# A recurrent mixer with an MLP on one core: v streamed twice in the diagonal products, new planner numbers, q and k loaded earlier

## The chip, the core and the metric

The kernel runs on one core of a Trainium2 chip. The metric is the time on the device of one execution, in microseconds (us). The engines of the core are TensorE (PE in the profile, its weight loads PEld), VectorE (DVE), ScalarE (ACT), GpSimd (POOL) and SyncE (SP), which issues nearly all DMAs here.

## What is computed

An mLSTM layer (4 batches, 8 heads, 768 steps, head width 40) is followed by a mixer over the sequence and an MLP of width 320 to 1280 to 320, all in float32.

```python
for t in range(S):
    m_new = np.maximum(f_gate[:, :, t] + m, i_gate[:, :, t])
    f_stab = np.exp(f_gate[:, :, t] + m - m_new)
    i_stab = np.exp(i_gate[:, :, t] - m_new)
    C = f_stab[..., None] * C + i_stab[..., None] * np.einsum('bhd,bhe->bhde', vt, kt)
    n = f_stab * n + i_stab * kt
    h_tilde = np.einsum('bhde,bhe->bhd', C, qt)
    denom = np.maximum(np.abs(np.einsum('bhd,bhd->bh', n, qt)[:, :, None]), 1.0)
    y[:, :, t] = o * h_tilde / denom          # o = sigmoid(o_gate)
u = x + (x.T @ U @ V).T                       # x: y with the heads side by side
out = u + np.maximum(u @ w_ch1, 0.0) @ w_ch2
```

## The kernel before, in words

The recurrence is computed in chunks of 128 steps. A sequence is cut into two halves of 384 steps (`hf`), a half into three chunks, and the heads into groups of 3, 3 and 2. `gates()` runs the scalar recurrence of all 32 rows once per half: a scan for m (`gate_max`, L415), the exponentials (`gate_exp`, `gate_input_exp` on ACT), two more scans (`gate_w` L445, `gate_g` L453), and small products on PE that turn the results (`gate_turn`, L466) and spread the totals (`totals`).

`attention(b, base)` does, for each head of a half:
- `scores`: k times q for three chunks, for two heads at once in the two halves of PE's rows, six matmuls with 40 rows and 128 columns each (in the trace `ps<-qk`, and each float32 matmul is two MATMUL records);
- `decay` (`ps<-fhl,idsel`) or `load_decay` (`fd<-fsd`, a DMA): a row of forget factors on all partitions;
- `decay_scan` (L779, DVE), which makes the 128x128 decay triangles, and `weigh` (L783, DVE), scores times decay into `wt`;
- `pv`: the diagonal products, three matmuls `ps<-tk,wt` with the weights `wt` (128 by 128) and v with a column of ones as the moving operand, 41 columns.

For each head group `kv` (`ps<-v,tk`) makes the state of each chunk, `kv_mask` (L699) and `state` (L713) carry it on, `inter` (`ps<-C,q`) adds what comes from earlier chunks, and `norm`, `out_norm` and `gate` write x. `rows` and `cols` apply U and V, and `mlp(b, hf)` runs ten row blocks of `up` (`ps<-ut,w1h` and `w1l`, 384 columns), `relu_high` (ACT L947), `relu_low` (DVE L949) and `down` (`ps<-w2h,h` and `w2l`, 320 columns). The MLP operands are split in a high and a low part; the weights are unpacked from float64 words by DVE (`weight_shift` L531, `weight_sign` L533, `weight_tail` L535).

The order on every engine is made by a planner (`Plan`) while the kernel is built. Each piece of work is an `op` with a priority, an engine, a cost and its dependencies; `ORDER` adds to the priority by kind, `ORDER0` adds more for batch 0 (`p.batch == 0`). Of what can start first on an engine, the piece with the lowest priority number is taken. SP issues the DMAs in this order, and a DMA whose buffer is still held blocks those behind it. `dma(nbytes)` gives the planned time of a transfer. Where the plan finds PE idle, or finds that PE would stream fewer than `TICK_COLUMNS` columns in a slice `TICK` of its time, `keep_busy` puts in fillers: matmuls of a tile of zeros, 256 columns of bf16 (`ps<-zeros`), that nobody reads. `load` tells the planner which share of a piece's time counts as streaming. The fillers are in the program as fixed instructions: if PE gets there late, they run all the same. Every matmul goes through the helper `mm`, so in the trace they all stand under L296.

```python
while FORCE:
    n = int(start // TICK)
    left = (n + 1) * TICK - start
    gain = 2.4 / (2 if start < COLD else 1)
    lack = TICK_COLUMNS - busy[n] - load * gain * min(cost, left)
    if lack <= gain * max(0.0, left - cost) or left < FILL_NS or not filler(start):
        break
```

Of the kernel before, what the change touches and what calls it, by code (L numbers as in the profile page):

```python
# [20 lines left out]
P = 128  # L21
# [3 lines left out]
DV = D + 1  # L25
# [19 lines left out]
BF_FROM = 64  # L45
LAG = 2
CV0, CV1, CV2 = 53.6, 80.0, 95.3
TICK, TICK_COLUMNS, FILL_NS, FILL_COLUMNS = 5120.0 / 3, 2000.0, 107.0, 256.0
RP, MP = 75.4, 175.5
GP = 21.3  # L50
ALT_PRI = 94.9
FILL_SLACK, FORCE, FILL_TO = 0.8, True, 4096.0

ORDER = {
    "gate": 20.0, "gate_w": 10.0, "part2": -70.0, "out_norm": -30.0, "part1": -10.0, "gate_turn": 10.0, "part3":
    -30.0, "rest1": 2.0, "w_low": 30.0, "vi": -10.0, "state": -4.0, "qk_low": -10.0, "load_tk": -20.0, "w13_low":
    -30.0,
}
ORDER0 = {
    "rows": 25.0, "inter": 3.0, "x_low": -10.0, "weigh": 10.0,  # L60
}
BEGIN, COLD = 600.0, 7000.0
DELTA = {"pe": 0}

WIDE_DMA = 630.0
PLAIN = 222.0


SLOTS = {
# [203 lines left out]
def mlstm_mixer_kernel(  # L273
# [21 lines left out]
    def mm(o, a, b, start=True, stop=True, **kw):  # L295
        nc.tensor.matmul(o, a, b, start=start, stop=stop, **kw)  # L296
# [4 lines left out]
    def grid(ap, *dims):  # L301

        n = 1
        for d in dims:
            n *= d
        ap = ap[:, 0:n]
        if len(dims) == 2:
            return ap.rearrange("p (a b) -> p a b", b=dims[1])
        if len(dims) == 3:
            return ap.rearrange("p (a b c) -> p a b c", b=dims[1], c=dims[2])  # L310
        return ap
# [31 lines left out]
    p = Plan(tiles)  # L343
    T = p.at
# [15 lines left out]
        return ("pool", "dve"), (pool(n), dve(n))  # L360

    def dma(nbytes):
        return nbytes / 360.0

    def gates():
        XF, G0, G1 = ("gx",), ("g0",), ("g1",)
# [263 lines left out]
    def attention(b, base):  # L630
# [5 lines left out]
        def at(n):  # L636
            return base + 88.6 * n / span
# [6 lines left out]
        def group(j, n):  # L644

            gi, hf = js[j]
            h0, nh = GROUPS[gi]
            r, wd = nh * D, nh * DV
# [6 lines left out]
            def vtv():  # L655
                return T[kt][:, o1:o2].rearrange("p (c h d) -> p c h d", c=3, d=DV)
# [7 lines left out]
            def load():  # L664
# [7 lines left out]
                w=[kq], new=[(kq, "q3")],  # L672
            )
            p.op("v2", at(n - 1), ("pool", "dve"), (pool(3 * wd) * 0.83, dve(3 * wd)), lambda e: e.tensor_mul(v2v(), vtv(), tokv(1, gi, hf, DV)),  # L674
                 r=[(kt, "v"), ("tok", hf, 1)], w=[kv2], new=[(kv2, "v2")])
            p.op("vi", at(n - 1), ("pool", "dve"), (pool(3 * wd) * 0.83, dve(3 * wd)), lambda e: e.tensor_mul(vtv(), vtv(), tokv(0, gi, hf, DV)),
                 r=[("tok", hf, 0)], w=[(kt, "v")])
            p.op("sigmoid", at(n - 1) + 3, "act", act(3 * r) + (1283 if b + j == 0 else 0), lambda: nc.scalar.activation(otv(), otv(), AF.Sigmoid),
                 r=[("exp", n) for n in range(4)], w=[(kt, "o")])
# [61 lines left out]
            for hh in range(nh):  # L741
                h = h0 + hh
                bh = b * NHEAD + h
                u = n + hh
                kdm, kw, kfb = [(s, b, hf, h) for s in ("dm", "wt", "fb")]
                kqk, ks = ("qk", b, hf, h // 2), ("sp", b, hf, h)
                if h % 2 == 0:
                    pair = [("sp", b, hf, h + i) for i in range(2)]
                    for i in range(2):
                        def load_qk(kqk=kqk, h=h, i=i):  # L750
                            nc.sync.dma_start(
                                out=T[kqk][64 * i:64 * i + D].rearrange("p n s -> p (n s)"), in_=qk[b, h + i, hf, 0:D],
                            )

                        p.op("load_qk", at(u) - 7, "sp", dma(D * 2 * HS * 4), load_qk, w=[(kqk, i)], new=[(kqk, "qk")] if i == 0 else [])

                    def scmm(pair=pair, kqk=kqk):
                        for c in range(3):
                            cs = slice(c * P, (c + 1) * P)
                            for i, ks in enumerate(pair):  # L760
                                rs = slice(64 * i, 64 * i + D)
                                mm(T[ks][:, cs], T[kqk][rs, 1, cs], T[kqk][rs, 0, cs])

                    p.op("scores", at(u), "pe", 3 * PLAIN, scmm, r=[(kqk, 0), (kqk, 1)], w=pair, new=[(ks, "at") for ks in pair], load=0.6)

                def fbmm(kfb=kfb, bh=bh):
                    mm(T[kfb][:, 0:HS], idsel[:, bh:bh + 1].to_broadcast([2 * NBH, P]), fhl[hf])

                def fbdma(kfb=kfb, bh=bh):
                    row = fsd[bh:bh + 1, hf * HS:(hf + 1) * HS]  # L770
                    nc.sync.dma_start(out=T[kfb], in_=row.to_broadcast([P, HS]))

                if u + 16 * b < FB_FROM:
                    p.op("decay", at(u), "pe", 190, fbmm, r=[("fhl", hf), ("fh", hf), ("idents",)], w=[kfb], new=[(kfb, "at")], load=0.42)
                else:
                    p.op("load_decay", at(u) - 6, "sp", dma(P * HS * 4), fbdma, r=[("fsd", hf)], w=[kfb], new=[(kfb, "fd")])
                p.op(
                    "decay_scan", at(u), "dve", scan(HS),
                    lambda kfb=kfb, kdm=kdm: nc.vector.tensor_tensor_scan(  # L779
                        T[kdm], T[kfb][:, 0:HS], ident3.rearrange("p c t -> p (c t)"), 0.0, ALU.mult, ALU.add),  # L780
                    r=[kfb, ("idents",)], w=[kdm], new=[(kdm, "dm")], lock=u + 16 * b >= FB_FROM,
                )
                p.op("weigh", at(u), "dve", dve(HS), lambda ks=ks, kw=kw, kdm=kdm: nc.vector.tensor_mul(T[kw], T[ks][:, 0:HS], T[kdm]),  # L783
                     r=[ks, kdm], w=[kw], new=[(kw, "wt")])

                kpb = ("pb", b, j, hh)
                if fine:
                    thirds(at(u + 0.5), lambda kw=kw: T[kw], lambda i, kpb=kpb: T[kpb][:, i, :], HS, kw, kpb, "pb")

                def pvmm(hh=hh, kw=kw, kpb=kpb):  # L790
                    num = grid(T[kn], 3, nh, DV)
                    if fine:
                        for c in range(3):
                            for n, (i, k) in enumerate(PARTS):
                                mm(
                                    num[:, c, hh, :], T[kpb][:, i, c * P:(c + 1) * P],
                                    T[kvb][:, k, 0:3 * wd].rearrange("p (c h d) -> p c h d", c=3, d=DV)[:, c, hh, :],
                                    start=(hh == 0 and c == 0 and n == 0), stop=(n == 5), skip_group_check=True,
                                )
                        return  # L800
                    for c in range(3):
                        mm(num[:, c, hh, :], T[kw][:, c * P:(c + 1) * P], vtv()[:, c, hh, :],
                           start=(hh == 0 and c == 0), skip_group_check=True)

                p.op(
                    "pv", at(u + 1), "pe", 460 if fine else 3 * PLAIN, pvmm,
                    r=[(k, i) for k in (kpb, kvb) for i in range(3)] if fine else [kw, (kt, "v")], w=[(kn, hh)],
                    new=[(kn, "st")] if hh == 0 else [], stream="att", load=0.65 if fine else 0.31,
                )

            pf = at(last + 0.2)
# [282 lines left out]
```

## Time and profile before

| | |
|---|---|
| median of 3 runs | 456.32 us (455.13 to 458.31) |
| the profiled execution | 458.37 us |
| its span, first to last instruction | 456.6 us |
| mean granted clock of TensorE over the span | 0.886 |
| PE, DVE, ACT, POOL busy | 430.2, 254.4, 123.7, 82.6 us |
| MATMUL records | 2839, of them 263 fillers (43.4 us busy) |
| bytes moved by DMA | 48.94 MB, mean 107 GB/s |

The span is what the trace shows; the 1.8 us between it and the execution's time lie around it. The granted clock is 1.0 at 2.4 GHz and 0.5 at 1.2 GHz. Busy PE time includes matmuls that run at either level.

### The profile page before, as it was taken

The page shows a single profiled execution, that of the slowest core. Times are in us where ns is not written, and L with a number is a line of the kernel's source. Part 1 is how long each engine was busy: PE and PEld are TensorE (multiplying, and loading weights), DVE is VectorE, ACT ScalarE, POOL GpSimd, SP SyncE. Part 2 cuts the span into 40 slices and gives each one's busy share as a digit, 9 for nine tenths or more (in the row PEclk, how much of TensorE's full clock was granted, in tenths as well). Part 3 has the DMA queues.
Part 4 walks back from the last instruction along what each step waited for, and adds up shares of the span by engine and source line. Part 5 has one row for each costly group of instructions (what it writes and reads, how often), then busy time and mean ns, then how long its engine had stood idle before and what let it go on. Part 6 is the DMA issues. An engine that isn't in the chain of part 4 may idle for free.

```text
span 456.6 us, 7500 instructions
## 1 busy us (share of the span) xinstructions
PE 430.2 (94%) x2839; PEld 402.9 (88%) x2839; DVE 254.4 (56%) x534; ACT 123.7 (27%) x317; POOL 82.6 (18%) x96
## 2 busy tenths in 40 slices
PE   7999999999978788999797989999999999999997
PEld 5787889987867787999796889999999999999996
DVE  6555546679888976525787966442583132321222
ACT  4411131256334344021033221321232122221120
POOL 1332453036023050000331332000120000000000
PEclk9555555599998999999999976999999999999999
DMA  8612535766695253202794764310100000000001
GB/s 248 186 48 77 170 103 139 245 212 194 192 271 167 78 152 108 76 14 94 209 224 137 230 182 126 108 45 0 51 23 0 1 13 31 32 12 1 14 30 43
DMA packets 27258, 48.94 MB, mean 107 GB/s; under 512 B 3864, under 2 KB 18840, under 8 KB 27224
## 3 DMA queue, kind: packets, MB, share of 16 engines
q1 hardware_dynamic: 27032, 48.08, 35.9%
q8 instruction: 22, 0.36, 0.3%
q10 hardware_dynamic: 192, 0.40, 0.3%
q14 instruction: 12, 0.10, 0.1%
HBM read 44.24 MB, written 4.23 MB: 106 GB/s over the span
## 4 chain that ended last, share of the span: by engine, by line
PE 74%; DMA 13%; DVE 9%; issue 2%; ACT 1%; SPq 1%; DVEq 0%; ACTq 0%
PE ps L296 73%; DMA fd<-fsd 6%; DMA tk<-in_tk 4%; DVE dm L779 3%; DMA qk<-in_qk 2%; DMA raw<-in_w 1%; DVE cv L535 1%; DVE cv L533 1%; DVE wt L783 1%; DMA q<-in_q 1%; DVE h L949 1%; DVE cv L531 0%; DVE C L713 0%; DVE o L972 0%; PE ps L466 0%
## 5 line engine op out<-in xcount | busy, mean ns | idle before, releaser
L296 PE MATMUL ps<-ut,w1h 128*128 128x384 f32 x400 | 123.5, 348 | 3.0 <-DVE h L949 2.9
L296 PE MATMUL ps<-w2h,h 128*128 128x320 f32 x480 | 121.6, 314 | 0.0
L949 DVE SCALAR_TENSOR_TENSOR h<-ps,h 128x384 fp32r<-128x384 f32 x80 | 43.8, 554 | 92.2 <-ACT h L947 91.8
L296 PEld LDWEIGHTS ps<-w2h,h 128*128 128x128 f32 x480 | 84.5, 190 | 0.5
L296 PE MATMUL ps<-ut,w1l 128*128 128x384 f32 x240 | 82.4, 343 | 0.0
L296 PEld LDWEIGHTS ps<-ut,w1h 128*128 128x128 f32 x400 | 75.7, 193 | 3.9 <-DVE h L949 3.6
L947 ACT ACTIVATE h<-ps 128x384 fp32r<-128x384 f32 x80 | 38.7, 490 | 147.0 <-PE ps L296 140.1
L296 PE MATMUL ps<-w2l,h 128*128 128x320 f32 x240 | 74.4, 310 | 1.0 <-DVE w2l L580 1.0
L296 PEld LDWEIGHTS ps<-tk,wt 128*128 128x128 f32 x384 | 62.0, 239 | 7.1 <-issue 4.6
L296 PE MATMUL ps<-tk,wt 128*128 128x41 f32 x384 | 62.8, 318 | 3.8 <-DVE wt L783 3.1
L779 DVE TENSOR_TENSOR_SCAN dm<-fd,ident 128x384 f32<-128x384 f32 x48 | 49.0, 1033 | 7.5 <-DMA fd<-fsd 7.5
L296 PE MATMUL ps<-zeros 128*128 128x256 bf16 x263 | 43.4, 314 | 8.7 <-DVE wt L783 4.7
L296 PEld LDWEIGHTS ps<-w2l,h 128*128 128x128 f32 x240 | 45.5, 190 | 1.3 <-DVE w2l L580 1.3
L296 PEld LDWEIGHTS ps<-ut,w1l 128*128 128x128 f32 x240 | 46.4, 193 | 0.0
L296 PEld LDWEIGHTS <-zeros 128*128 128x128 bf16 x263 | 27.9, 113 | 18.7 <-issue 10.7
L296 PE MATMUL ps<-qk 40*128 40x128 f32 x384 | 38.6, 342 | 2.2 <-DMA qk<-in_qk 2.2
L674 POOL TENSOR_TENSOR v<-tk,tok 128x369 f32<-128x369 f32 (+1 forms) x20 | 15.9, 793 | 129.6 <-PE ps L296 88.0
L783 DVE TENSOR_TENSOR wt<-ps,dm 128x384 f32<-128x384 f32 x64 | 33.8, 543 | 7.9 <-PE ps L296 7.7
L296 PEld LDWEIGHTS ps<-qk 40*128 40x128 f32 x384 | 31.4, 234 | 7.7 <-DMA qk<-in_qk 2.8
L699 ACT ACTIVATE C<-ps,cst 120x123 f32<-120x123 f32 (+3 forms) x58 | 16.1, 344 | 50.0 <-PE ps L296 48.2
L779 DVE TENSOR_TENSOR_SCAN dm<-ps,ident 128x384 f32<-128x384 f32 x16 | 14.9, 950 | 17.8 <-PE ps L296 17.8
L972 DVE TENSOR_TENSOR o<-ps,x 128x320 f32<-128x320 f32 x24 | 11.3, 490 | 23.3 <-PE ps L296 23.3
(95 smaller groups left out, 447.1 us busy)
## 6 DMA issues: line engine op xcount, KB each, us to landing
fd<-fsd SPq DMA_DIRECT2D x48, 192.0 KB
tk<-in_tk SPq DMA_DIRECT2D x16, 544.5 KB
qk<-in_qk SPq DMA_DIRECT2D x64, 120.0 KB
raw<-in_w SPq DMA_DIRECT2D x20, 320.0 KB
out<-o SPq DMA_DIRECT2D x24, 160.0 KB
tk<-in_tk SPq DMA_DIRECT2D x8, 363.0 KB
q<-in_q SPq DMA_DIRECT2D x16, 180.0 KB
fd<-gsd SPq DMA_DIRECT2D x12, 120.0 KB
```

What stands on the lines that cost most here:

```text
L296: nc.tensor.matmul(o, a, b, start=start, stop=stop, **kw)
L533: p.op("weight_sign", pri, "dve", dve(n), lambda tu=tu, hi=hi: V.scalar_tensor_tensor(tu(), hi(), 0x80000000, tu(), ALU.bitwise_and, ALU.b ...
L535: p.op("weight_tail", pri, "dve", dve(n), lambda tu=tu, lo=lo: V.scalar_tensor_tensor(tu(), lo(), 29, tu(), ALU.logical_shift_right, ALU.b ...
L674: p.op("v2", at(n - 1), ("pool", "dve"), (pool(3 * wd) * 0.83, dve(3 * wd)), lambda e: e.tensor_mul(v2v(), vtv(), tokv(1, gi, hf, DV)), r= ...
L699: nc.scalar.activation(grid(T[kc], 3, wd)[0:r, 0:nk, hs], ps[:, :, hs], AF.Copy, scale=col)
L779: lambda kfb=kfb, kdm=kdm: nc.vector.tensor_tensor_scan(T[kdm], T[kfb][:, 0:HS], ident3.rearrange("p c t -> p (c t)"), 0.0, ALU.mult, ALU. ...
L783: p.op("weigh", at(u), "dve", dve(HS), lambda ks=ks, kw=kw, kdm=kdm: nc.vector.tensor_mul(T[kw], T[ks][:, 0:HS], T[kdm]), r=[ks, kdm], w=[ ...
L947: p.op("relu_high", pri + m - 1000, "act", 371, lambda: nc.scalar.activation(T[kh][:, 0, :], T[kp][:, 0:HS], AF.Relu), r=[kp], w=[(kh, 0)] ...
L949: p.op("relu_low", pri + m - 1000, "dve", dve(HS), lambda: nc.vector.scalar_tensor_tensor(T[kh][:, 1, :], T[kp][:, 0:HS], 0.0, f32(T[kh][: ...
L972: p.op("residual", pri - 1000, "dve", dve(DM), lambda: nc.vector.tensor_add(T[ko], T[ka][:, 0:DM], T[X][:, tt, 0:DM]), r=[ka] + [(X, hf, g ...
```

## The change

The numbers of the planner change: more columns per slice (2400 for 2000), a transfer rate of 270 for 360, other priorities by kind for all batches and for batch 0, and other priorities for the mixer's rows and columns (`RP`, `MP`). `scores` is planned 200 ns longer with the same streamed columns. In the instructions themselves one thing changes: in `pv` v's 41 columns are given twice as the moving operand, and the second result goes to a spare place of the same PSUM bank that nobody reads. All line numbers move down by 5 to 7.

```diff
-TICK, TICK_COLUMNS, FILL_NS, FILL_COLUMNS = 5120.0 / 3, 2000.0, 107.0, 256.0
-RP, MP = 75.4, 175.5
+TICK, TICK_COLUMNS, FILL_NS, FILL_COLUMNS = 5120.0 / 3, 2400.0, 107.0, 256.0
+RP, MP = 80.1, 170.7
-ALT_PRI = 94.9
+ALT_PRI = 85.9
-    "gate": 20.0, "gate_w": 10.0, "part2": -70.0, ... "qk_low": -10.0, "load_tk": -20.0, ...
+    "gate": 20.0, "gate_w": 7.3, "part2": -70.0, ... "load_tk": -20.0, "load_qk": 0.9,
+    "load_decay": -20.3, "w13_low": -30.0, "x_low": 24.0, "rows": -12.2, "inter": -1.6, "weigh": 1.8, ...
 ORDER0 = {
-    "rows": 25.0, "inter": 3.0, "x_low": -10.0, "weigh": 10.0,
+    "gate_w": 19.3, "part3": -44.0, "load_tk": 17.0, "load_q": -1.4, "x_low": -10.0, "rows": 25.0, ...
+SPARE = 9
     def dma(nbytes):
-        return nbytes / 360.0
+        return nbytes / 270.0
-p.op("scores", at(u), "pe", 3 * PLAIN, scmm, ..., load=0.6)
+p.op("scores", at(u), "pe", 3 * PLAIN + 200, scmm, ..., load=0.46)
-                        mm(num[:, c, hh, :], T[kw][:, c * P:(c + 1) * P], vtv()[:, c, hh, :],
+                        s = c * nh + hh
+                        twice = grid(T[kn], SPARE + 1, DV)[:, s:SPARE + 1:SPARE - s]
+                        mm(twice, T[kw][:, c * P:(c + 1) * P], vtv()[:, c, hh, :].unsqueeze(1).to_broadcast([P, 2, DV]),
                            start=(hh == 0 and c == 0), skip_group_check=True)
-                    new=[(kn, "st")] if hh == 0 else [], stream="att", load=0.65 if fine else 0.31,
+                    new=[(kn, "st")] if hh == 0 else [], stream="att", load=0.65 if fine else 0.6,
```

Three places show what the new numbers do to the order. The first is the start of SP's queue; `in_tk` carries k, v and the output gates, `in_qk` q and k for the scores, `in_q` q for the state's part. Before:

```order
L377 DMA x_82<-in_fig 32x768
L666 DMA tk_95<-in_tk 128x1089
L666 DMA tk_96<-in_tk 128x1089
L751 DMA qk_107<-in_qk 40x768 x2
L671 DMA q_0_100<-in_q 120x384
L666 DMA tk_97<-in_tk 128x726
L751 DMA qk_108<-in_qk 40x768 x2
```

And now:

```order
L382 DMA x_82<-in_fig 32x768
L671 DMA tk_95<-in_tk 128x1089
L676 DMA q_0_100<-in_q 120x384
L756 DMA qk_107<-in_qk 40x768 x2
L671 DMA tk_96<-in_tk 128x1089
L756 DMA qk_108<-in_qk 40x768 x2
```

The second block of k, v and gates now stands behind the first q and k, and a block of q ahead of them.

The second place is PE just behind the first scores and their fillers. `x_83,cst` is `totals`, `cst,x_84` is `gate_turn` of the result of `gate_w`, `fhl_67,idsel` is `decay`, `qk_108` the next scores. Before:

```order
L296 MATMUL ps_137<-x_83,cst 120x12 x2
L296 MATMUL ps_137<-x_83,cst 80x12
L296 MATMUL ps_138<-fhl_67,idsel 128x384
L296 MATMUL ps_139<-fhl_67,idsel 128x384
L466 MATMUL ps_134<-cst,x_84 128x32 x3
L296 MATMUL ps_140<-qk_108 128x128
```

And now:

```order
L301 MATMUL ps_137<-x_83,cst 120x12 x2
L301 MATMUL ps_137<-x_83,cst 80x12
L471 MATMUL ps_134<-cst,x_84 128x32 x3
L301 MATMUL ps_138<-fhl_67,idsel 128x384
L301 MATMUL ps_139<-fhl_67,idsel 128x384
L301 LDWEIGHTS zeros
L301 MATMUL ps_137<-zeros 128x256
```

The turn of `gate_w` has moved ahead of the two decays, and seven fillers follow them (one stands here) where the next scores stood.

The third place is DVE in the same stretch; `x_82`, `x_83`, `x_84` hold the gates, the second line of each fence and its like are scans of 384 steps. Before:

```order
L415 SCALAR_TENSOR_TENSOR x_83<-x_82,x_83 32x384
L427 COPY x_82<-x_83 32x3
L428 MEMSET x_83 32x3
L418 TENSOR_TENSOR x_82<-x_82,x_83 32x384
L453 SCALAR_TENSOR_TENSOR x_84<-x_83,x_82 32x384
L445 SCALAR_TENSOR_TENSOR x_84<-x_83,x_82 32x384
L477 TENSOR_TENSOR x_83<-x_84,cst 32x12
L434 TENSOR_TENSOR fhl_67<-x_83,fhl_67 32x384
L450 TENSOR_TENSOR x_84<-x_84,x_82 32x384
```

And now:

```order
L432 COPY x_82<-x_83 32x3
L433 MEMSET x_83 32x3
L458 SCALAR_TENSOR_TENSOR x_84<-x_83,x_82 32x384
L420 SCALAR_TENSOR_TENSOR x_83<-x_82,x_83 32x384
L482 TENSOR_TENSOR x_83<-x_84,cst 32x12
L450 SCALAR_TENSOR_TENSOR x_84<-x_83,x_82 32x384
L439 TENSOR_TENSOR fhl_67<-x_83,fhl_67 32x384
L455 TENSOR_TENSOR x_84<-x_84,x_82 32x384
```

The scan of the second half (L415, now L420) has moved behind `gate_g` of the first (L453, now L458), and the subtraction L418 of the second half has left the stretch.

In the whole program the fillers go from 263 to 222. Ahead of the first `up` stand 200 (155 before) with the same 78 score, 66 pv and 24 kv matmuls; the longest runs of fillers there are 22, 23, 15, 14 and 14 in place of 18 and 32. Up to the ninth `relu_low` it is 222 fillers (246 before). The run of 22 stands behind 179 other matmuls; before, the seven of 92.31 us in the trace stood behind 203. DVE has 164 instructions ahead of the first `relu_low` (145 before) and 234 ahead of the ninth (265 before). Every other count of instructions is as it was.

## Rows read from the trace of the kernel before

**Rows 1.** The page, part 2: busy tenths and granted clock in 40 slices
```profile
PE   7999999999978788999797989999999999999997
...
PEclk9555555599998999999999976999999999999999
```

**Rows 2.** Stretches: us, busy us by engine (instructions), granted clock, DMA share, GB/s
```profile
core 0: us, PE busy (x) PEld busy (x) DVE busy (x) ACT busy (x) POOL busy (x), PEclk, DMA share, GB/s
0.00:11.55 11.55, 8.17 (x56) 5.96 (x56) 7.84 (x18) 5.08 (x10) 1.92 (x8) 1.00 0.85 247
11.55:93.47 81.92, 81.92 (x410) 69.55 (x408) 45.76 (x95) 19.63 (x62) 26.14 (x32) 0.50 0.47 139
93.47:107.40 13.93, 13.55 (x128) 11.85 (x127) 11.99 (x29) 8.14 (x20) 7.30 (x6) 1.00 0.68 211
...
0.00:172.63 172.63, 157.62 (x986) 136.90 (x986) 121.98 (x265) 59.47 (x160) 53.17 (x64) 0.75 0.57 167
93.47:137.84 44.37, 39.27 (x335) 35.09 (x334) 39.79 (x90) 21.18 (x53) 14.28 (x14) 1.00 0.73 217
```

**Rows 3.** The chain of work that ended last: start us, us, what
```profile
2.58 7.48 DMA qk<-in_qk
```

**Rows 4.** PE in order of time, from 6.7: start us, us, instruction, [idle before]
```profile
6.71 0.72 PE L296 MATMUL ps<-zeros 128*128 128x256 bf16 x5
9.05 0.48 PE L296 MATMUL ps<-qk 40*128 40x128 f32 x2 [1.62 <-DMA qk<-in_qk]
10.10 0.93 PE L296 MATMUL ps<-qk 40*128 40x128 f32 x10 [0.57 <-DMA qk<-in_qk]
10.97 0.94 PE L296 MATMUL ps<-zeros 128*128 128x256 bf16 x6
11.83 1.24 PE L296 MATMUL ps<-x,cst 32*120 32x12 f32 x6
```

**Rows 5.** DVE in order of time, the first gates
```profile
8.48 0.94 DVE L453 TENSOR_TENSOR_SCAN x<-x,x 32x384 f32<-32x384 f32 x1
...
10.94 0.55 DVE L450 TENSOR_TENSOR x<-x,x 32x384 f32<-32x384 f32 x1
```

**Rows 6.** PE's groups by shape from 11.55 to 93.47: count, busy us, mean ns
```profile
L296 PE MATMUL ps<-tk,wt 128*128 128x41 f32 x114 | 26.3, 403 | 0.0
...
L296 PE MATMUL ps<-zeros 128*128 128x256 bf16 x55 | 14.8, 408 | 0.0
```

**Rows 7.** The same view from 93.47 to 226.5
```profile
L296 PE MATMUL ps<-tk,wt 128*128 128x41 f32 x132 | 17.1, 273 | 3.0 <-DVE wt L783 2.8 <-DVE tk L676 0.2
...
L296 PE MATMUL ps<-v,tk 128*120 128x123 f32 x24 | 3.6, 279 | 0.0
...
L296 PE MATMUL ps<-v,tk 128*80 128x82 f32 x16 | 1.7, 241 | 0.0
```

**Rows 8.** PE in order of time, fillers late in the front
```profile
92.31 1.51 PE L296 MATMUL ps<-zeros 128*128 128x256 bf16 x7
...
102.69 3.67 PE L296 MATMUL ps<-zeros 128*128 128x256 bf16 x32
```

**Rows 9.** Stretches with columns as in rows 2, the later ones at half clock
```profile
137.84:141.26 3.42, 3.10 (x14) 2.73 (x14) 3.42 (x5) 1.68 (x4) 2.90 (x3) 0.50 0.78 206
226.59:230.00 3.41, 3.41 (x14) 3.41 (x14) 2.48 (x5) 0.88 (x2) 1.81 (x2) 0.50 0.76 225
267.55:281.20 13.65, 13.65 (x64) 13.28 (x63) 7.72 (x16) 2.77 (x9) 6.47 (x8) 0.50 0.57 164
```

**Rows 10.** PE in order of time, the waits near them
```profile
138.16 1.65 PE L296 MATMUL ps<-zeros 128*128 128x256 bf16 x7 [3.62 <-DVE wt L783]
...
225.83 0.83 PE L296 MATMUL ps<-tk,wt 128*128 128x41 f32 x6 [2.40 <-DVE wt L783]
226.49 0.58 PE L296 MATMUL ps<-ut,w1h 128*128 128x384 f32 x1
...
266.89 0.42 PE L296 MATMUL ps<-h,u 128*128 128x320 f32 x1 [1.34 <-DVE h L872]
```

More of the change, by code (lines that the diff above doesn't have):

```diff
@@ L47 @@
 CV0, CV1, CV2 = 53.6, 80.0, 95.3
-TICK, TICK_COLUMNS, FILL_NS, FILL_COLUMNS = 5120.0 / 3, 2000.0, 107.0, 256.0
-RP, MP = 75.4, 175.5
+TICK, TICK_COLUMNS, FILL_NS, FILL_COLUMNS = 5120.0 / 3, 2400.0, 107.0, 256.0
+RP, MP = 80.1, 170.7
 GP = 21.3
-ALT_PRI = 94.9
+ALT_PRI = 85.9
 FILL_SLACK, FORCE, FILL_TO = 0.8, True, 4096.0
 ORDER = {
-    "gate": 20.0, "gate_w": 10.0, "part2": -70.0, "out_norm": -30.0, "part1": -10.0, "gate_turn": 10.0, "part3":
-    -30.0, "rest1": 2.0, "w_low": 30.0, "vi": -10.0, "state": -4.0, "qk_low": -10.0, "load_tk": -20.0, "w13_low":
-    -30.0,
+    "gate": 20.0, "gate_w": 7.3, "part2": -70.0, "out_norm": -30.0, "part1": -10.0, "gate_turn": 10.0,
+    "part3": -10.6, "rest1": 2.0, "w_low": 30.0, "vi": -10.0, "state": -4.0, "load_tk": -20.0, "load_qk": 0.9,
+    "load_decay": -20.3, "w13_low": -30.0, "x_low": 24.0, "rows": -12.2, "inter": -1.6, "weigh": 1.8,
+    "scores": 1.7, "weight_sign": -24.3, "weight_tail": 4.3, "cols": 21.8, "ut_high": 32.4, "store": 5.0,
+    "decay_exp": -0.1,
 }
 ORDER0 = {
-    "rows": 25.0, "inter": 3.0, "x_low": -10.0, "weigh": 10.0,
+    "gate_w": 19.3, "part3": -44.0, "load_tk": 17.0, "load_q": -1.4, "x_low": -10.0, "rows": 25.0, "inter":
+    -27.5, "weigh": 10.0, "scores": -4.1, "q_decay": 2.8, "weight_rebase": -20.9, "weight_sign": -23.3,
+    "cols": 32.8, "store_g": 32.7, "residual": -7.0, "w_high": -27.4,
 }
@@ L762, in scmm @@
                                 mm(T[ks][:, cs], T[kqk][rs, 1, cs], T[kqk][rs, 0, cs])
-                    p.op("scores", at(u), "pe", 3 * PLAIN, scmm, r=[(kqk, 0), (kqk, 1)], w=pair, new=[(ks, "at") for ks in pair], load=0.6)
+                    p.op("scores", at(u), "pe", 3 * PLAIN + 200, scmm, r=[(kqk, 0), (kqk, 1)], w=pair, new=[(ks, "at") for ks in pair], load=0.46)
                 def fbmm(kfb=kfb, bh=bh):
```

## The prediction

> **What bounds the kernel now.** I read the page's slices first. PE is at 9 tenths in nearly every slice, but its granted clock reads 5 in seven slices near the start [rows 1]. The stretches give the edges: from 11.55 to 93.47 us, 81.92 us long, PE is busy all the time and the granted clock is 0.50, the lower of its two levels; DVE is busy 45.76 us of it, the DMA engines 0.47 [rows 2]. So in this stretch PE alone sets the pace, at half speed. Behind it, from 93.47 to 137.84, PE has its full clock, DVE is busy 39.79 of 44.37 us and the DMA share is 0.73 [rows 2]: there the other engines bind. Three more stretches run at half clock, 3.42, 3.41 and 13.65 us, 20.48 together [rows 9].
>
> What came before the fall is seen in PE's order of time. Its five fillers end at 7.43, then PE waits 1.62 us for the first q and k and, after two records, 0.57 us for the second head's: 2.19 us, and it fills 10.06 to 12 with thin work [rows 4]. The chain of waits has the same transfer, 7.48 us long, ending at 10.06 [rows 3]. The later falls also follow waits: 3.62 us at 138, 2.40 at 226, 1.34 at 267 [rows 10]. What came before the rise: at 92.31 seven fillers in a row [rows 8]. Between, PE was never idle and yet the clock stayed low. Most of the records there are narrow: 114 stream 41 columns (26.3 of the 81.92 us) [rows 6].
>
> **The change part by part.** *The first q and k.* In SP's queue two blocks of k, v and gates stood ahead of them (2 x 128 x 1089 x 4 bytes, 1115 KB); now one block and a q (558 + 184 KB) do, 373 KB less. At the 247 GB/s of this stretch [rows 2] that is 1.5 us: the two heads land at about 7.6 and 8.6 instead of 9.05 and 10.06. PE has eight fillers in place of five, which end at 7.43 + 3 x 0.115 = 7.8 (0.115 us is 3.67 / 32, a filler at full clock [rows 8]). The wait shrinks from 2.19 us to some 0.8 (estimate).
>
> *What is late next.* Scores (0.9 us), seven fillers (0.8) and `totals` (0.6, half of the 1.24 at half clock [rows 4]) bring PE to about 10.9. Its next piece turns `gate_w`'s product, which DVE ended at 10.94 + 0.55 = 11.49 before [rows 5]. On DVE a scan of the second half has moved in, one subtraction has gone, and the chain may start before the 8.48 at which its first scan stood [rows 5], so it ends at 11.0 to 11.5: a wait of 0.1 to 0.6 us. Queued behind it on PE are two decays and seven fillers, and DVE's first decay scans wait for these decays. So the single pause of 2.19 us becomes two short ones with 1.7 us of dense work between. I take it that this no longer brings the clock down in most executions, and keep the other case as a rival, because no row shows the smallest pause that does.
>
> *The clock.* The same PE work at full clock takes half: 81.92 / 2 = **-41.0 us**. It counts fully only if nobody else needs the time. I test that at the ninth `relu_low`, at 172.6, where DVE has done 265 instructions in 121.98 busy us [rows 2]. PE alone: 157.62 busy - 41.0 - 1.7 (the first short fall) - 24 fillers fewer x 0.115 = 112 us. DVE: now 31 instructions fewer stand ahead, x 0.46 us mean (121.98 / 265) = 14.3; 107.7 us, at the 0.897 that it reaches in 93.47 to 137.84 it needs 120. DMA: 0.57 x 172.63 = 98.4 us of full use; at the share 0.85 of the first stretch 116 us, at 0.73 135 us [rows 2]. So the point can't come before about 116 and need not come after 135. The clock's gain puts it at 129 (172.6 - 41.0 - 1.7 - 0.7, the last two terms below), inside. Bounds: 13 us more, 6 us less.
>
> *Fillers.* 45 more ahead of the first `up` (+5.2 us), 24 fewer up to the ninth `relu_low` (-2.8). A filler in a wait costs nothing. The cover is the floors of DVE and DMA (120 and up to 135 us), which lie above PE's 112. I take 0; without cover -2.8 to +5.2.
>
> *v twice.* 384 records stream 82 columns in place of 41. At full clock records of 41 columns take 17.1 us / 132 = 0.130 us each, of 82 columns 1.7 / 16 = 0.106, of 123 columns 3.6 / 24 = 0.150 [rows 7]. So the price is between nothing and 384 x 0.020 = 7.7 us; the row with the same columns is the nearest and says nothing: the weight load is what paces them. I take 0.
>
> *The start.* q and k come 1.5 us earlier, but `gate_w` holds PE again: between 0 and -1.4, I take **-0.7**.
>
> *Later falls.* 20.48 us at half clock are worth 10.2 us at most [rows 9]. Each follows a wait for DVE, and behind those stand transfers that the slower planned rate may or may not put right. With wider records and the first short fall's stage loosened I take one of the three away: **-1.7**; bounds -10.2 and, with one more as long as the longest, +6.8.
>
> Sum, against the profiled execution's own 458.4 us (span 456.6): 458.4 - 41.0 - 1.7 - 0.7 = **415.0 us**. The median of the runs shown is 2.0 us lower than that execution, so the forecast may be 2 us high.
>
> **A rule of the Trainium skill against the row.** PE is busy all of 81.92 us and the granted clock stays at 0.50 [rows 2]. The Trainium skill, TensorE: Matmul & The Clock Gate, section "What's actually happening", says that the throttled clock is the default, that activity releases it and that the gate goes by how busy PE has been recently. Taken as busy time the trace disagrees (100% busy, not released); taken as streamed work it does not. By the rule in busy time v twice would buy nothing after a fall, and rival 2 would come out as rival 3; by the row, narrow records held the clock down, and wider ones help it up.
>
> **The rivals.** *1, the forecast: no lasting fall in the front, 415 (400 to 428).* For it: the wait at the start is cut to a third, v twice doubles the columns in the largest group of the stretch [rows 6]. Against it: a new wait for `gate_w`. Chance 0.60.
>
> *2, the clock still falls in the first 15 us but rises early, after 15 to 40 us.* For it: fillers in sevens and tens with state products between them come soon after the start, and seven in a row stood at the rise at 92.31 [rows 8]. It gives back 7.5 to 20 us: 422 to 435, say 428. Chance 0.20.
>
> *3, the change doesn't do it: the fall stays until the long run of 22 fillers.* That run stands 24 matmuls earlier than the seven of 92.31 did, at half clock about 0.4 us each (81.92 less 55 fillers at 0.27 us [rows 6] over 175 matmuls), so the low stretch ends some 9.6 us earlier, worth 4.8; the 45 more fillers take back up to 5.2. About 455. Chance 0.11.
>
> *4, slower: the low clock lasts to the first `up`.* Place: the front's end. There PE is the bound, so fillers cost directly: the 13.55 us that ran at full clock from 93.47 to 107.40 [rows 2] take twice as long, +13.6, and 45 more fillers at 2 x 0.115 are +10.4; DVE's 31 fewer instructions give at most 14.3 back later. 468 to 482. It is decided by whether runs of 14 to 23 fillers raise the clock; seven did [rows 8], so it is unlikely. Chance 0.05.
>
> *5, as 1, but more is gained:* the floors' near end and no later falls, 390 to 400. For it: DVE's and DMA's floors at 116 to 120. Against it: waits of 3.62 and 2.40 us come at just such shares [rows 9, 10]. Chance 0.04.
>
> **How the numbers follow.** The likeliest is rival 1, so 415. 400 to 428 holds most of its 0.60; with rival 2 taken in, up to 440, the range has about 0.80. Outside lie 3 and 4 (0.16) and 5 (0.04). One per cent is about what a measurement of this kernel can tell from no change: 456.3 less 1% is 451.8. Faster: 1, 2, 5 = 0.84, of which I take 0.01 off for the ends: 0.83. Same: most of 3, 0.09. Slower: 4 and the upper part of 3, 0.08.
>
> **What would show it.** In the changed profile the slices 2 to 8 should read 9 in the clock's row, the stretch to the first `up` should be some 36 us shorter, with DVE near 90% busy in it, and PE's two first waits should read about 0.8 (for q and k) and under 0.6 us (for `gate_w`). The `pv` records should keep their 0.13 us at full clock. DMA's share in the first 60 us should be over 0.7. If the slices read 5 from 11 us on and turn to 9 before 50, rival 2 holds; if they turn only at 85 or later, 3 or 4. I am wrong about the floors if the clock is full and the ninth `relu_low` still comes after 140: then transfers or DVE took the gain.

## The result and the profile after

The changed kernel takes 418.41 us (median of 4 executions, 414.5 to 422.14) beside 456.91 us of the kernel before (4 executions, 455.13 to 458.31): a ratio of 0.913 with a 95% interval of 0.904 to 0.922. The forecast was 415.0, with a range of 400 to 440. The profiled execution took 416.58 us, its span is 414.8 us, its mean granted clock 0.970.

Executions of one kernel here differ in where PE's clock falls, so times below stand with the mean granted clock of their execution. The ratios leave out executions over 1.5% above the fastest of their kernel, so they can differ from the quotient of the medians.

| | before | after |
|---|---|---|
| span of the profiled execution | 456.6 us | 414.8 us |
| PE busy, PE idle (span less busy) | 430.2, 26.4 us | 393.2, 21.6 us |
| at half clock: ahead of the first `up`, behind it | 81.92, 20.48 us | 23.90, 0 us |
| first `up` on PE | 107.4 us | 93.8 us |
| ninth `relu_low` on DVE | 172.6 us | 132.0 us |
| from there to the end | 284.0 us | 282.8 us |

The page of after, parts 1 and 2: busy time of each engine, then PE's busy tenths and its granted clock in 40 slices of 10.4 us.

```profile
PE 393.2 (95%) x2798; PEld 368.5 (89%) x2798; DVE 258.1 (62%) x534; ACT 124.6 (30%) x317; POOL 82.6 (20%) x96
...
PE   7995999998989999998899999999999999999995
...
PEclk9999558999999999999999999999999999999999
```

Where [rows 1] had seven slices of 5 from the second slice on, there are two, the fifth and the sixth. The later falls of [rows 9] are gone altogether. The stretches of after, columns as in [rows 2]:

```profile
0.00:41.59 41.59, 34.05 (x285) 27.66 (x286) 32.56 (x70) 14.81 (x39) 15.83 (x25) 1.00 0.67 188
41.59:65.49 23.90, 23.90 (x118) 20.13 (x117) 15.07 (x28) 5.76 (x17) 10.05 (x13) 0.50 0.73 194
65.49:92.70 27.21, 25.75 (x234) 22.16 (x234) 25.43 (x56) 13.67 (x38) 6.91 (x8) 1.00 0.71 217
92.70:132.00 39.30, 35.74 (x249) 32.18 (x248) 38.78 (x80) 19.26 (x47) 14.20 (x14) 1.00 0.78 217
0.00:93.80 93.80, 84.66 (x638) 70.67 (x638) 74.07 (x157) 35.34 (x97) 32.80 (x45) 0.87 0.70 197
0.00:132.00 132.00, 119.43 (x879) 102.13 (x880) 111.84 (x233) 53.49 (x140) 47.00 (x59) 0.91 0.72 204
```

The clock is full for 41.59 us, where before it had fallen at 11.55. Then it is at 0.50 for 23.90 us, with PE busy all of them. In the last stretch ahead of the ninth `relu_low` DVE is busy 38.78 of 39.30 us and PE 35.74: there DVE sets the pace. PE of after in order of time (start, us, instruction, idle before it and what ended that):

```profile
8.25 1.56 PE L301 MATMUL ps<-qk 40*128 40x128 f32 x12 [0.15 <-DMA qk<-in_qk]
...
11.57 0.37 PE L471 MATMUL ps<-cst,x 32*128 32x32 f32 x3 [0.24 <-DVE x L455]
...
41.33 0.96 PE L301 MATMUL ps<-v,tk 128*120 128x123 f32 x4 [4.23 <-POOL v L679]
...
66.31 2.58 PE L301 MATMUL ps<-zeros 128*128 128x256 bf16 x22
```

The 2.19 us for q and k [rows 4] are 0.15, and the turn of `gate_w` waits 0.24. A wait that the kernel before did not have stands just before the fall: 4.23 us for a product that POOL makes of the fifth block of k, v and gates. The chain of waits has that block:

```profile
29.08 11.25 DMA tk<-in_tk
...
40.47 0.81 POOL v L679
...
41.33 24.20 PE ps L301 x116
```

The transfer is issued at 29.08, takes 11.25 us and holds POOL, and PE with it, until 41.3. The rise at 65.49 came before the long run of 22 fillers at 66.31, behind doubled `pv` records and state products (`ps<-v,tk`).

### The profile page after: what moved, and what is told of

It reads as the page before. It is cut to its first block, busy times and chain, and to the rows that moved or that the text cites. A ratio compares the mean times of both kernels' runs of the same rounds, so it can differ in the third digit from the quotient of the medians.

```text
span 414.8 us, 7420 instructions
## 1 busy us (share of the span) xinstructions
PE 393.2 (95%) x2798; PEld 368.5 (89%) x2798; DVE 258.1 (62%) x534; ACT 124.6 (30%) x317; POOL 82.6 (20%) x96
## 3 DMA queue, kind: packets, MB, share of 16 engines
HBM read 44.24 MB, written 4.23 MB: 117 GB/s over the span
## 4 chain that ended last, share of the span: by engine, by line
PE 66%; DVE 16%; DMA 10%; issue 4%; ACT 1%; SPq 0%; POOL 0%; DVEq 0%; POOLq 0%; ACTq 0%
PE ps L301 66%; DMA tk<-in_tk 5%; DVE dm L784 4%; DMA q<-in_q 2%; DVE wt L788 2%; DMA qk<-in_qk 2%; DVE cv L538 1%; DMA raw<-in_w 1%; DVE cv L540 1%; DVE C L718 1%; DVE h L956 1%; DVE cv L536 1%; ACT C L704 0%; DVE x L450 0%; DVE q L732 0%
## 5 line engine op out<-in xcount | busy, mean ns | idle before, releaser
L301 PE MATMUL ps<-ut,w1h 128*128 128x384 f32 x400 | 120.9, 342 | 0.6 <-DVE h L956 0.4
L301 PE MATMUL ps<-ut,w1l 128*128 128x384 f32 x240 | 80.7, 336 | 0.0
L301 PEld LDWEIGHTS ps<-ut,w1h 128*128 128x128 f32 x400 | 73.7, 188 | 1.8 <-DVE h L956 0.7
L301 PE MATMUL ps<-tk,wt 128*128 128x82 f32 x384 | 55.0, 287 | 6.0 <-DVE wt L788 5.4
L301 PEld LDWEIGHTS ps<-tk,wt 128*128 128x128 f32 x384 | 51.2, 204 | 10.3 <-DVE wt L788 7.8
L301 PE MATMUL ps<-qk 40*128 40x128 f32 x384 | 33.9, 304 | 1.1 <-DVE dm L784 0.8
L301 PEld LDWEIGHTS ps<-qk 40*128 40x128 f32 x384 | 27.2, 199 | 6.6 <-issue 1.9
L301 PE MATMUL ps<-zeros 128*128 128x256 bf16 x222 | 31.5, 287 | 1.6 <-DVE x L415 1.1
L301 PEld LDWEIGHTS <-zeros 128*128 128x128 bf16 x222 | 21.3, 103 | 7.3 <-issue 1.8
L301 PE MATMUL ps<-v,tk 128*120 128x123 f32 (+1 forms) x120 | 17.3, 278 | 4.5 <-POOL v L679 4.2
```

## Two lines: the clock, and the order

Before the experiments, the reading that sorts them. Plotted as time against mean granted clock, the executions lie near straight lines. The kernel before (31 executions, run beside the experiments, 433.12 us at 0.948 to 460.91 at 0.88): 442.1 us at 0.93, and 3.15 us less for each 0.01 of clock, with a scatter of 1.8 us. The kernel after (8 executions, 413.12 at 0.968 to 433.48 at 0.909): 427.1 us at 0.93, and 3.18 us for each 0.01. So the lines are parallel, 15.0 us apart. Single executions at like clocks say the same without a line: 431.76 us of after at 0.914 (c1) beside 446.93 of before at 0.916, and 445.3 us of f1 at 0.872 beside 457.7, 459.25 and 460.37 of before at 0.873. I worked out the last column below by such a line through each kernel's own executions; it is an estimate from few points.

| kernel | order of work | v | us at granted clock | at 0.93 |
|---|---|---|---|---|
| c3_twice_alone | of before | twice | 445.59 at 0.911, 444.53 at 0.927, 442.85 at 0.941, 443.34 at 0.945 | 444 |
| c4_qk_first_alone | of before, q and k first | once | 456.38 at 0.879, 458.19 at 0.884, 451.9 at 0.9, 437.14 at 0.944 | 442 |
| f2_columns_alone | re-planned, 2400 columns | once | ten, 458.98 at 0.862 to 447.35 at 0.92 | 444 |
| f1_rate_270_alone | re-planned, rate 270 | once | 445.3 at 0.872, 433.28 at 0.901, 426.48 and 427.37 at 0.924 | 424 |
| c2_v_once | of after | once | 430.66 at 0.916, 426.95 at 0.928, 423.11 at 0.931, 421.71 at 0.939 | 425 |
| d1_old_start | of after, second block ahead of q and k | twice | 427.47 and 427.33 at 0.934, 425.38 at 0.938, 420.97 at 0.958 | 428 |
| c1_after_again | of after | twice | 433.48 at 0.909, 431.76 at 0.914, 413.12 and 413.33 at 0.968 | 426 |

Every kernel of the table falls on one of two levels: 442 to 444 us, or 424 to 428. What puts it on the lower level is the order that comes with the planned rate of 270: f1 has nothing else. The doubled v and the early q and k change, as far as four executions each can tell, where on its line a kernel lies. The lines have two limits. Nearly all executions of d2, d3, d4 and f3 lie at 0.96 and above, too far from 0.93 for the table. And the mean clock does not say where in the kernel the half clock fell: f4, with 417.73 us at 0.941, lies some 6 us below the line of after.

## The experiments

### After once more, and the two parts undone or done alone

*c1_after_again*: the kernel after, unchanged.

> The changed kernel once more, on the chip that the next three run on. 414 to 422 us, ratio to the kernel before 0.905 to 0.925; in the profile no half-clock stretch before 35 us, and one of 15 to 30 us behind the 4.23 us wait for the block of k, v and gates at 37 to 41 us.

Median 422.55 us, 0.911 of before (0.906 to 0.917), with two executions at 413 and two at 432 and 433. So executions at 432 and 433 us, and the place of the fall, missed what I expected. The profile of c1 (413.33 us) is at half clock at other places than the first one: from 27.20 to 44.27 and from 57.92 to 64.75, 23.90 us together, and it has no wait for POOL's product. So the 4.23 us wait isn't needed for a fall; the same instructions in the same order lose the clock at different places.

*c2_v_once*: after, with v once.

```diff
-                        mm(twice, T[kw][:, c * P:(c + 1) * P], vtv()[:, c, hh, :].unsqueeze(1).to_broadcast([P, 2, DV]),
+                        mm(num[:, c, hh, :], T[kw][:, c * P:(c + 1) * P], vtv()[:, c, hh, :],
```

> The changed kernel with v streamed once (41 columns) and every instruction in the same place. Theory (wide records keep the clock up and help it rise, and cost nothing): the clock falls earlier, at 15 to 30 us, or rises later than at 65.5, so that the half-clock time in the front grows from 24 us to 35 to 60, and the kernel takes 424 to 440 us. Rival (early q and k and the fillers did it, v twice does nothing): the same 24 us at half clock, 414 to 422 us. If v twice cost PE time at full clock, v once would be faster by up to 7 us.

Median 425.03 us, 0.935 (0.927 to 0.943). Its stretches:

```profile
27.90:72.27 44.37, 44.37 (x222) 37.15 (x222) 27.42 (x57) 9.77 (x28) 15.50 (x20) 0.50 0.67 181
...
0.00:137.00 137.00, 129.23 (x879) 110.42 (x880) 110.24 (x233) 53.26 (x140) 47.21 (x59) 0.83 0.68 196
```

In these two profiles the same 879 PE records up to the ninth `relu_low` need 137.00 us in place of 132.00, with 44.37 us at half clock in place of 23.90. One profile each doesn't settle it: the four executions of c2 lie at 421.71 to 430.66 us, those of c1 at 413.12 to 433.48, and the medians, 425.03 and 422.55, are closer than either spread. At the same granted clock c2 and after agree (425 against 426 to 428): so the second 41 columns cost nothing measurable, and what they gain comes through the clock. That they do gain is shown by the next run.

*c3_twice_alone*: before, with v twice and nothing else.

```diff
-                        mm(num[:, c, hh, :], T[kw][:, c * P:(c + 1) * P], vtv()[:, c, hh, :],
+                        mm(twice, T[kw][:, c * P:(c + 1) * P], vtv()[:, c, hh, :].unsqueeze(1).to_broadcast([P, 2, DV]),
```

> The kernel before with v streamed twice, every instruction in the old place, so with the old wait of 2.2 us for the first q and k. Theory: the clock still falls at about 11.5 us, but rises before 60 us, since the low clock was held by narrow records: 425 to 445 us. Rival (only the missing wait counts): low until about 93 us as before, 453 to 460 us.

Median 443.93 us, 0.980 (0.975 to 0.984). The first fall stays, but ends early, and another one follows:

```profile
12.91:33.39 20.48, 20.48 (x103) 17.04 (x103) 11.75 (x23) 6.87 (x20) 7.86 (x10) 0.50 0.38 118
47.04:81.17 34.13, 34.04 (x175) 30.31 (x176) 19.78 (x42) 8.38 (x25) 13.13 (x16) 0.50 0.64 179
0.00:161.70 161.70, 147.38 (x986) 128.44 (x986) 120.81 (x265) 60.21 (x160) 53.57 (x64) 0.81 0.64 178
```

With the order of before and wider records the long stretch of 81.92 us breaks in two of 54.6 together. All four executions are faster than the seven of before beside them (451.75 to 458.92 us), at clocks of 0.911 to 0.945 against 0.879 to 0.894; beside other runs single executions of before came to 433 to 447 us. The two executions with the highest clock, 0.941 and 0.945, are some 5 us over the line of before; why the clock bought less there stays open.

*c4_qk_first_alone*: before, with the second block of k, v and gates issued behind the first q and k.

```diff
+                if (b, j) == (0, 1):
+                    later.append(go)
...
+                            while i == 1 and later:
+                                later.pop()()
```

> The kernel before with one DMA moved: the second block of k, v and gates is issued behind the first two q and k transfers. All else in the old place. Theory: the first wait goes from 2.2 us to about 1, the fall at 11.5 us is put off at most to the next thin place (before 40 us), and with narrow records the clock then stays low until about 85 to 93 us: 445 to 458 us. Rival (the wait at the start is the whole cause): no fall in the front, 410 to 425 us.

Median 454.14 us beside 453.97 of before. PE in order of time, and the stretch behind:

```profile
7.59 1.45 PE L296 MATMUL ps<-qk 40*128 40x128 f32 x12
...
10.60 0.73 PE L296 MATMUL ps<-x,cst 32*120 32x12 f32 x6 [0.80 <-DVE x L477]
```

```profile
12.43:90.94 78.51, 78.51 (x390) 67.06 (x390) 44.39 (x92) 18.35 (x56) 26.45 (x32) 0.50 0.49 140
```

The wait for q and k is gone, and in its place `totals` on PE waits 0.80 us for DVE; three of its four executions stay at clocks of 0.879 to 0.9, and one reached 437.14 us at 0.944. By itself the early load shows no gain in these four.

*d1_old_start*: after, with the second block back ahead of q and k.

```diff
+                if (b, j) == (0, 1):
+                    return
+                if (b, j) == (0, 0):
+                    nc.sync.dma_start(out=tiles["tk"][1][:, 0:cn], in_=tk[b, hf, :, cn:2 * cn])
```

> The changed kernel with one DMA moved back: the second block of k, v and gates is issued right behind the first, ahead of the first q and k; all else stays. Theory (the early q and k prevent the first fall, v twice then gets the clock up again): the wait for q and k is back at 1.5 to 2.5 us, the clock falls at 11 to 14 us and rises before 45, half-clock time in the front 20 to 50 us: 420 to 440 us. Rival (the place of q and k does not matter): 412 to 422 us as the changed kernel.

Median 426.36 us. (For the runs of this group of kernels no ratio is given, because the executions of before beside them spread from 433.12 to 460.91.) PE waits 1.83 and 0.33 us for q and k again, and:

```profile
10.71:65.32 54.61, 54.61 (x275) 45.26 (x276) 28.40 (x61) 12.35 (x39) 20.51 (x26) 0.50 0.49 135
...
0.00:142.50 142.50, 132.52 (x879) 112.80 (x880) 109.31 (x234) 53.44 (x140) 46.49 (x59) 0.81 0.67 189
```

In the profile the fall is back, at 10.71. By the medians the old start costs 4 to 8 us (426.36 beside 422.55 of c1 and 418.41 of the first four of after), less than the spread of after itself, and no execution of after ran beside d1. So that the early q and k are worth something in the new order is likely, and their price is not shown. My figure for the rise (before 45) was wrong, it came at 65.32.

### The wait for the fifth block, and denser streaming

*d2_block_early*: after, with the fifth block of k, v and gates in a buffer of its own, issued ahead of the second store of the gates; two unused buffers are dropped for it.

```diff
+    ahead = const.tile([P, 3 * 3 * (2 * D + DV)], F32, name="ahead")
+    p.fixed["tk", 0, 4] = ahead
...
+            nc.sync.dma_start(out=ahead[:, 0:3 * w], in_=tk[0, 1, :, 3 * w:6 * w])
```

> The changed kernel with one more buffer, so that the fifth block of k, v and gates, which held PE for 4.23 us at 37 to 41 us in the first profile, is issued some 10 us earlier (ahead of the second store of g); every other instruction in its place. Theory (the fall at 41.6 us came from that wait): no such wait, half-clock time in the front under 12 us in the profile, 400 to 408 us. Rival (thin places elsewhere bring the clock down as well, as at 27.2 us in the repeated profile, where that wait did not occur): still 15 to 30 us at half clock in some executions, 408 to 422 us.

Median 415.19 us (425.45 at 0.931, the others 413.75 to 415.25 at 0.963 to 0.974). I had expected 400 to 408: missed. The wait is gone, and the best executions are those of after. The profiled one (425.45) even lost the clock from 13.59 to 71.62, 58.03 us with v doubled, and from 7 us on PE had waited no longer than 0.26 us before it fell. So the 4.23 us wait was one occasion for a fall, not the thing that holds the kernel at 414.

*d3_fillers_at_scores* and *d4_both*: after, with four fillers behind each pair of score matmuls in batch 0 (32 more in the trace, 254 for 222; I had counted 36); d4 has d2's early block as well.

```diff
+                        if b == 0 or (b, hf, h) == (1, 0, 0):
+                            for _ in range(4):
+                                p.warm(float("inf"))
```

> The changed kernel with four more fillers behind each pair of scores of batch 0 and the first pair of batch 1 (36 more, 4.1 us of PE at full clock). Theory (the thin stretches around the 40-row scores bring the clock down; denser streaming there holds it): no fall before the wait for the fifth block, at most a short one behind it, 404 to 414 us, and the executions lie closer together. Rival (the fillers only cost): 416 to 424 us with the same half-clock time.

> The early fifth block and the 36 fillers together. Theory: no half-clock stretch in the front in most executions, 398 to 406 us. Rival (the other engines bind once the clock holds, by the floors of the prediction): full clock, and yet 406 to 414 us.

Medians 416.08 and 415.95 us; all 12 executions lie between 414.69 and 418.84, at clocks of 0.966 to 0.983. My theories missed (404 to 414 for d3, 398 to 406 for d4); the rival of d4, that other engines bind once the clock holds, missed by 2 us only. Streaming more takes away the bad executions (after had 422, 432 and 433 among its eight, in other runs) and does not better the good ones. The stretches of d4:

```profile
57.20:67.50 10.30, 10.30 (x53) 8.56 (x54) 8.45 (x17) 2.98 (x8) 3.56 (x4) 0.50 0.90 265
92.00:131.20 39.20, 34.53 (x241) 31.49 (x242) 37.50 (x77) 18.10 (x45) 14.27 (x14) 1.00 0.74 215
```

Half clock is down to 10.30 us in the front, 13.60 less than in after, and the ninth `relu_low` comes at 131.2 instead of 132.0. So the clock that came back buys hardly anything: ahead of that point DVE is busy 37.50 of 39.20 us.

### The planner's numbers alone

*f1_rate_270_alone* and *f2_columns_alone*: before, with one planner number each.

```diff
-        return nbytes / 360.0
+        return nbytes / 270.0
```

```diff
-TICK, TICK_COLUMNS, FILL_NS, FILL_COLUMNS = 5120.0 / 3, 2000.0, 107.0, 256.0
+TICK, TICK_COLUMNS, FILL_NS, FILL_COLUMNS = 5120.0 / 3, 2400.0, 107.0, 256.0
```

> The kernel before with one planner number changed: a planned transfer rate of 270 for 360. q and k still stand behind two blocks of k, v and gates, and v is streamed once; the order is re-planned, 199 fillers instead of 263 (157 before the first up, where 155 were). My theory (early q and k and the doubled v lift the clock, not the planner's numbers by themselves): the first fall stays near 12 us and lasts to 80 or later, 445 to 462 us. Rival (the slower planned rate by itself puts the later waits and falls right): no half clock after 110 us, at most the 10.2 us of the later falls gained: 440 to 448 us, and the fall in the front as before.

> The kernel before with one planner number changed: 2400 columns per slice for 2000. 297 fillers instead of 263 (179 before the first up, where 155 were), v streamed once, q and k behind two blocks. My theory: denser planned slices raise the clock earlier but not at once, as the first wait of 2.2 us stays: fall near 12 us, rise between 50 and 85 us, 435 to 455 us. Rival (more fillers only lengthen the half-clock stretch): rise at 90 or later, 455 to 465 us.

f1: 430.32 us beside 454.85 of before, 0.952 (0.940 to 0.963). f2: 450.3 us beside the same 454.85, 0.999 (0.991 to 1.008). For f1 both expectations missed: I held the rate for a side matter, and by itself it brings about half of the whole gain. Its profiled execution (445.3 us at 0.872) shows how, since its clock is worse than that of before:

```profile
12.04:100.78 88.74, 87.78 (x435) 73.82 (x435) 55.56 (x116) 23.82 (x69) 29.42 (x36) 0.50 0.51 151
...
0.00:160.30 160.30, 149.67 (x867) 129.28 (x868) 112.58 (x243) 54.54 (x145) 49.28 (x60) 0.68 0.57 170
...
160.30:443.30 283.00, 275.96 (x1911) 269.46 (x1909) 141.80 (x289) 69.59 (x172) 36.92 (x41) 0.98 0.27 77
```

The same stretch of before, and of after:

```profile
172.63:456.60 283.97, 272.59 (x1853) 266.03 (x1853) 132.40 (x271) 64.21 (x157) 29.48 (x32) 0.97 0.24 71
```

```profile
132.00:414.80 282.80, 273.75 (x1920) 266.38 (x1920) 146.21 (x302) 71.09 (x178) 35.62 (x37) 1.00 0.27 78
```

f1 has 88.74 us at half clock in the front where before had 81.92, and still its ninth `relu_low` comes at 160.3 instead of 172.6. Ahead of it stand 867 PE records for 986 (61 of the 119 fewer are fillers) and 243 DVE instructions for 265, 9.4 us less of DVE (112.58 against 121.98 [rows 2]). The DVE work is done behind it, where PE has the MLP to do and DVE is busy half the time (132.40 of 283.97 us, now 141.80 of 283.00), so there it costs nothing: 283.0 us against 284.0. Over the whole span PE's idle time goes from 26.4 to 17.7 us (443.3 - 425.6), and the fillers from 263 to 199, 64 x 0.115 = 7.4 us at full clock [rows 8]. Together 16 us, about the distance of the two lines; this is an account from one profile each, not a test. The number of fillers alone is an unlikely cause: f2 has 297 and stays on the upper line with before's 263, and leaving out 54 changes nothing in f3 below. After moves the same kind of work: 233 DVE instructions and 879 records ahead of the point, 146.21 us of DVE behind it. So the order is shown as the cause of the lower line, and the relief of DVE ahead of the point is my reading of how. Which of the moved pieces matter most wasn't tried, nor the changed priorities alone.

For f2 the theory came out in substance: the time of before, and a fall near 12 us that a rise at 18.7 breaks and a second, longer fall follows, up to 80.

### The fixed fillers

*f3_half_late_fillers* and *f4_no_late_fillers*: d4, with every second one (f3) or all (f4, shown) of the last 108 fillers ahead of the first `up` left out.

```diff
+                    p.fillers += 1
+                    if not (122 <= p.fillers <= 229):
+                        mm(bank[:, 0:256], zeros[:, 0:P], zeros)
```

> The kernel d4_both (after, with the fifth block's transfer early and 32 fillers more at the first score pairs) less every second one of the 108 fillers that stand last before the first up: 54 fillers of 0.115 us, 6.2 us of PE's time at full clock. Theory of the floors (in the front DVE and the transfers bind, so fixed fillers cost nothing): the ninth relu_low stays at 131, 414 to 418 us. Rival (with the clock at full the fixed fillers hold the front's end, where PE is busy 23.30 of 24.50 us in d4_both and 11.6 of them are fillers): first up some 6 us earlier, ninth relu_low at 125 to 128, 409 to 413 us. Third: thinner streaming lets the clock fall, 418 to 428 us with a fall between 60 and 100.

> As f3_half_late_fillers, but all 108 of these fillers left out, 12.4 us of PE's time at full clock. Theory of the floors: 414 to 418 us, ninth relu_low at 131. Rival (fillers hold the front's end): first up 8 to 12 us earlier, ninth relu_low at 119 to 125, where DVE, 110.58 us busy up to it, would be at 0.9 or more: 402 to 409 us. Third: the clock falls in the thin stretch before the first up, 418 to 435 us.

Medians 415.26 us (414.44 to 416.96) and 417.13 us (414.08 to 419.22), beside 415.95 of d4. The floors' theory holds: 54 fillers cost nothing that can be measured. Without all 108 the clock is worse, and even that costs little:

```profile
70.29:90.77 20.48, 17.23 (x80) 14.94 (x80) 18.02 (x43) 8.35 (x23) 3.41 (x4) 0.50 0.74 218
...
0.00:129.90 129.90, 113.39 (x804) 96.51 (x805) 110.57 (x234) 53.36 (x140) 47.36 (x59) 0.89 0.72 207
```

Half clock returns for 20.48 us (and some 7 us ahead of them, where the mean clock over 70.29 us is 0.95). In the 20.48 us DVE is busy 18.02: there a slow PE delays hardly anything, and the ninth `relu_low` stays at 129.9. None of the versions run beats after's best executions; d3, d4 and f3 only spare its bad ones.

## Why the prediction was right, and where its steps were not

**The time** was met (415.0 for 418.41, or for 416.58 of the profiled execution), and so was the sign. The sum of 43.4 us saved stands against 41.8 measured (458.37 - 416.58). But the terms that make it are not the ones that made the gain, so that the sum came out is in part luck.

**The first waits.** Forecast 0.8 us for q and k and 0.1 to 0.6 for `gate_w`; measured 0.15 and 0.24, and no fall in the first 15 us. What it is worth is less clear: alone the early load shows no gain (c4), and taken back it costs 4 to 8 us by the medians, within the spread of after (d1).

**"No lasting fall in the front."** Wrong by place: the clock fell at 41.59 for 23.90 us. I looked for what would be late next at `gate_w` and did not follow the fifth block of k, v and gates, which is issued at 29.08 and takes 11.25 us. Nor does a fall need a pause like that, as c1 and d2 show. The execution lies between rival 1 and rival 2. Executions at 0.91 (431.76 and 433.48) are rival 2 in its price, 422 to 435; no profile shows where they lost the clock.

**The clock term**, -41.0, is the step that was mis-sized. It halved 81.92 us. Measured, the half-clock time of the front went down by 58.0 us and that of the later falls by all 20.48, where I had taken one of three away (-1.7, with -10.2 as its bound). Halved, these are 29.0 + 10.2 = 39.2 us. Yet by the line of before, 0.970 - 0.886 = 0.084 of clock is worth 0.084 x 315 = 26.5 us: a microsecond at half clock gave back about a third of itself (26.5 / 78.5), not half. This is an estimate, and it carries the line beyond before's best clock, 0.948. The profiles of d4 and f4 point to the reason: with the clock at full DVE takes over as the bound.

**The order** had no term at all. I counted the 31 DVE instructions fewer ahead of the ninth `relu_low` only for a floor, and the slower planned rate only under the later falls. By the two lines it is worth 15.0 us, and f1 has it without the rest. 26.5 + 15.0 = 41.5 us, beside the measured 41.8. So the forecast came right because what it claimed too much for the clock was about what it left out for the order. That the two are of one size is luck.

**The floors** at the ninth `relu_low` were nearly right, and they are the part of the forecast that was not luck: the 31 DVE instructions stood in them. Forecast 129 between 116 and 135, measured 132.0. PE's busy time was to be 112 and was 119.43; half of the 23.90 us at half clock more than accounts for it. DVE's was to be 107.7 and is 111.84, the transfers' full use 98.4 and is 0.72 x 132.0 = 95.0. DVE's rate over the whole stretch is 0.85 and not 0.897.

**The first `up`** was to come some 36 us earlier and came 13.6 us earlier, and DVE ahead of it was to be near 0.9 busy and is at 0.79 (74.07 of 93.80). I took the clock term as it stood and only took the fillers off it. The new order puts more DVE work ahead of the first `up` (157 instructions in 74.07 us, before 65.6 us) and less between it and the ninth `relu_low`. So the gain appears there: 38.2 us after the first `up` for 65.2.

**What raises the clock.** Rivals 2 and 4 rest on the seven fillers at the rise. But nine stood in the same low stretch of before, and the clock stayed at half:

```profile
15.98 2.10 PE L296 MATMUL ps<-zeros 128*128 128x256 bf16 x9
```

So a run of fillers at the rise did not show that such a run brings it about. In after the rise came ahead of the run of 22; in d4 it came at 67.50, near the end of that run. The reading that wider records help the clock up is borne out by c3, but they do not keep a long fall away: d2 was at half clock for 58.03 us with v doubled.

**v twice at nothing:** held. The `pv` records of after from 65.49 to 200 (busy us, mean ns, idle):

```profile
L301 PE MATMUL ps<-tk,wt 128*128 128x82 f32 x162 | 21.6, 274 | 3.3 <-DVE wt L788 2.8 <-DVE rd L834 0.3 <-DVE rd L836 0.2
```

21.6 / 162 = 0.133 us each, for 0.130 with 41 columns [rows 7]; over 384 records some 1.5 us. What it buys is shown by c3 (0.980 alone); c2 points the same way but does not settle it.

**Fillers at nothing:** held (f3). **The transfers** were to be above a share of 0.7 in the first 60 us; they are at 0.67 up to 41.59 and at 0.73 up to 65.49.

## What to carry to other kernels

When a change moves the order as well as the clock, give the order a term of its own: count per engine what leaves the stretch where that engine binds, and see whether it lands where the engine has room. Value a stretch at half clock by what the next engine lets you take back, not by half its length. Where executions of one kernel differ by the granted clock, lay several of them against it: two kernels are then compared at equal clock, and one profile is not taken for the kernel.

## What the runs showed of the hardware

The same program loses the clock at different places: after at 41.59 in one execution, at 27.20 and again at 57.92 in another. In d2 it fell at 13.59, where from 7 us on PE had waited 0.26 us at most; c1 had the like (0.19 us) and kept its clock there. Records of 128 by 128 weights in float32 take 0.133 us with 82 columns and 0.130 with 41, so the second 41 were nearly free. In the order of before they raised the granted clock of four executions to 0.911 to 0.945, where the seven of before beside them had 0.879 to 0.894 (c3). What exactly brings the clock down in one execution and not in the next is left open.
